# An attention and mixture-of-experts kernel: early table load, sums that hold their 1e-9, a first weight load in halves, and attention dealt out in shorter runs

## The chip, the cores and the metric

The kernel runs on one core of a Trainium2 chip, as one program. The metric is the device time of one execution in microseconds; of the kernel before there are three runs. The engines are called PE (TensorE, matrix products), ACT (ScalarE), DVE (VectorE), POOL (GpSimd) and SP (SyncE, which issues the DMAs).

## The reference

Attention over 4 batches, 8 heads, 576 positions of 64 channels, and behind it a layer of four experts over its output, weighted with given probabilities:

```python
scores = scale * np.matmul(q, k.transpose(0, 1, 3, 2))
mask_local = (rel >= 0) & (rel < stride)                       # heads 0 to 3, stride 32
mask_strided = (rel >= 0) & (pos[None, :] % stride == pos[:, None] % stride)   # heads 4 to 7
scores = np.where(masks[None, :, :, :], scores, -1000000000.0)
scores = scores - np.max(scores, axis=-1, keepdims=True)
attn = np.exp(scores)
attn = attn / (np.sum(attn, axis=-1, keepdims=True) + 1e-09)
x = np.matmul(attn, v)                                         # as 2304 rows of 512
p = domain_probs / (domain_probs.sum(-1, keepdims=True) + 1e-9)
for e in range(4):
    h = np.maximum(x @ w1[e], 0.0)                             # 512 to 1024
    out += p[:, e:e + 1] * (h @ w2[e])                         # 1024 to 512
```

## The kernel before

**Numbers.** Every fp32 operand of the expert layer is split into a high part (a copy by ACT) and a low part (source minus high part, by DVE or POOL), and each product is three products: high by high, low by high, high by low.

**Stages.** There are eight units: four experts, each with two halves of 512 hidden columns. Stage one computes attention and, in the same stretch, all eight units for the first 384 rows of x: line 752 multiplies with w1 (48 products of 384 columns for each unit), line 768 with w2 (36 of 512 columns). Stage two (from the first product of line 921) takes the next 896 rows through the units, stage three the last 1024, both with fewer products by sums of quarters (tiles s1 to s4 of the weights, t1 to t4 of x). The transforms of x for stage two (`plan_x`, line 895 and the sums of lines 667 and 670) need all of attention.

**Attention.** Sixteen pairs of heads come in the order local, strided, local, strided of each batch. A pair has two groups. For each group: scores on PE (line 494 local, 499 strided), mask and maximum on DVE (510, 513), the difference on DVE or POOL (516), the exponent on ACT (520), the sum on DVE (525 and 526 local, 528 strided), the reciprocal (529), the product with it on DVE or POOL (532), transposes on PE (556) which ACT or DVE copy out (433, 435), and products with v on PE (583 local, 591 strided). The result goes to `xh` and `xl` for the first 384 rows and to `xr1`, `xr2` for the others. In the strided tiles a 55th column holds 1e-9 and the sum reads it along; the local ones get the 1e-9 added in an instruction of its own (526).

**What sets the order.** No loop runs the work in its written order: `Plan.add` gathers operations with an engine, a length, the tokens that they read and write, and a due time; `Plan.walk` deals them out engine by engine, by the due times and by its own lengths. Pair n of attention has the due time `ZB * n` for the first four and `ZP * n` later, unit u has `Z0 + ZU * u`. On PE, products of the expert layer and attention take turns; once attention has run for `ROW` microseconds by the plan, it is the products' turn. Where PE would have nothing, `fill` puts in products of a zero tile (line 1232), of which nobody reads the result. The engines then run these fixed orders, with semaphores between them.

**Loads.** SP issues them one after another: q and k (422, 424), v (429), weights (652: a quarter of a w1 or w2 pair, 1 MB).

Of the kernel before, what the change touches and what calls it, by code (L numbers as in the profile page):

```python
# [8 lines left out]
F32 = mybir.dt.float32  # L9
# [18 lines left out]

# [4 lines left out]
class Plan:  # L33
# [5 lines left out]
    TICK = 4096 / 1200  # L39
    BUSY, WARM = 3200, 2000  # L40
    LANES, RING = 8, 2048
    DEEP = 1.3
    ROW = 1.51
    ENGINES = ("PE", "ACT", "DVE", "POOL", "SP")
    FLEX = {"VP": ("DVE", "POOL"), "AD": ("ACT", "DVE")}

# [263 lines left out]
def attn_moe_kernel(  # L310
# [48 lines left out]
    prs = const.tile([P, NTT, E], F32, name="prs")  # L359
    psums = const.tile([P, NTT], F32, name="psums")  # L360
    wz = const.tile([P, 512], BF16, name="wz")
    const.tile([P, 8], F32, name="skew")

    wt = {n: big.tile([P, 2, 2, 256], F32R, name=n) for n in QUART[:3] + ("s3",)}
    wq = {n: (t[:, 0], t[:, 1]) for n, t in wt.items()}
# [75 lines left out]
    def plan_pair(n):  # L441
# [16 lines left out]

        pmx = pm[kd][bf]

        def pmv(g0, g1):
            if kd == "S":
                return pmx[:, g0:g1, 0:W]
            a = pmx[:, P * g0 + 1:P * g0 + 2]
            return bass.AP(a.tensor, a.offset, [list(a.ap[0]), [3 * P, (g1 - g0) // 3], [P + 32, 3], [1, W]])

        def per(a, g0, g1):

# [5 lines left out]
        def rows(a, g0, g1):  # L474
            a = a[:, par, g0:g1]
            return a if kd == "S" else a.rearrange("p (v r) -> p v r", r=3)
        par = n % 2
        for gi, (g0, g1) in enumerate(GRP[kd]):
            z = zg[gi]
            ng = g1 - g0  # L480
            key = ("sc", n, "b", gi)
            nel = ng * W

            def scores(key=key, gi=gi, g0=g0, g1=g1):
                s = bank(key)
                for g in range(g0, g1):
                    o = (g - g0) * W
                    for h in range(2):
                        a = slice(64 * h, 64 * h + 64)
                        if kd == "L":  # L490
                            o0, nq, _ = QKL[gi]
                            for i in range(2):
                                t = o0 + 96 * (2 * ((g - g0) // 3) + i) + 32 * (g % 3)
                                nc.tensor.matmul(  # L494
                                    s[64 * h + 32 * i:64 * h + 32 * i + 32, o:o + W], qkv[a, t:t + 32],
                                    qkv[a, t + nq + 1:t + nq + 1 + W], start=True, stop=True)
                        else:
# [24 lines left out]
            def rsum(g0=g0, g1=g1):  # L522
                r = sm[:, par, g0:g1]
                if kd == "L":
                    nc.vector.tensor_reduce(out=rows(sm, g0, g1), in_=pmv(g0, g1), op=ALU.add, axis=AX.X)
                    nc.vector.tensor_scalar_add(out=r, in0=r, scalar1=1e-9)
                else:
                    nc.vector.tensor_reduce(out=r, in_=pmx[:, g0:g1, 0:W + 1], op=ALU.add, axis=AX.X)
                nc.vector.reciprocal(out=r, in_=r)

            def norm(e, g0=g0, g1=g1, ng=ng):
                engine(e).tensor_tensor(
                    out=pmv(g0, g1), in0=pmv(g0, g1), in1=per(sm, g0, g1), op=ALU.mult)

            tok, tm, ts = f"pm{kd}{bf}{gi}", f"mx{par}{gi}", f"sm{par}{gi}"
            dd = nel / 960 + 0.15
            vp = (dd, nel * 1.6e-3 + 0.22)
            add("PE", 0.2 + ng * (0.107, 0.116)[c > 1], scores, [f"qk{kd}{bf}{gi}"], [key, tok], z + 3, key, cols=(4, 2)[c > 1] * nel)
            add("DVE", dd, mask, [key, "mask" + kd], [tok], z + 3.2)
            add("DVE", dd, rmax, [tok], [tm], z + 3.4)  # L540
            add("VP", vp, bsub, [tm], [tok], z + 3.6)
            add("ACT", nel / 1200 + 0.2, ex, (), [tok], z + 3.8)
            add("DVE", dd + (0.45, 0.25)[c > 1], rsum, [tok], [ts], z + 4)
            add("VP", vp, norm, [ts], [tok], z + 4.2)


# [99 lines left out]
    units = [(e, f) for e in range(E) for f in range(F // FH)]  # L646
    NU = len(units)

    def load_w(which, u):
        e, f = units[u]  # L650
        src = w1[e, :, f * FH:(f + 1) * FH] if which == 1 else w2[e, f * FH:(f + 1) * FH, :]
        nc.sync.dma_start(out=raws[which], in_=src.rearrange("(k p) f -> p k f", p=P))

    def raw_quarter(i, j, which=1):
        return raws[which][:, 2 * j:2 * j + 2, 256 * i:256 * i + 256]
# [14 lines left out]
        add("VP", VP, lambda e: engine(e).tensor_tensor(out=dst(), in0=a(), in1=b(), op=ALU.add), toks, [tok], z)  # L670

    def plan_load(which, u, z):
        add("SP", 0.4, lambda: load_w(which, u), (), [f"raw{which}"], z, xfer=((2.9, 512),), lag=LAG)

    def plan_w2(z):
        for i in range(NKF):
            split(lambda i=i: raws[2][:, i, :], "raw2", lambda i=i: w2h[i], lambda i=i: w2l[i], f"w2{i}", z)

    A11, A12, A21, A22 = ((lambda i=i, j=j: raw_quarter(i, j)) for i in range(2) for j in range(2))

    def plan_quarter(src, tok, nm, z):
        split(src, tok, lambda: wq[nm][0], lambda: wq[nm][1], nm, z)

    def plan_w1_plain(z):
        for src, nm in ((A11, "a11"), (A12, "a12"), (A21, "s3"), (A22, "a22")):
            plan_quarter(src, "raw1", nm, z)

    tmp = {}

    def plan_w1(z, step, plain):  # L690

        def t(i):
            return lambda: tmp["s", i]

        if plain:
            plan_quarter(A11, "raw1", "a11", z)
        total(t(0), A21, A22, ["raw1"], "ws0", z + step)
        plan_quarter(t(0), "ws0", "s1", z + step)
        combine(t(1), t(0), A11, ["raw1", "ws0"], "ws1", z + 2 * step)
        plan_quarter(t(1), "ws1", "s2", z + 2 * step)  # L700
        if plain:
            plan_quarter(A12, "raw1", "a12", z + 3 * step)
        combine(t(2), A11, A21, ["raw1"], "ws2", z + 4 * step)
        plan_quarter(t(2), "ws2", "s3", z + 4 * step)
        if plain:
            plan_quarter(A22, "raw1", "a22", z + 5 * step)
        combine(t(0), A12, t(1), ["raw1", "ws1"], "ws0", z + 6 * step)
        plan_quarter(t(0), "ws0", "s4", z + 6 * step)


# [7 lines left out]
    def plan_keep2(u, z, step):  # L718
# [8 lines left out]
        def t(i):  # L727
            return lambda: tmp["s", i]
# [4 lines left out]
            add("SP", 0.4, lambda: nc.sync.dma_start(out=d2[u, nm], in_=late["wv"][v].bitcast(F32)), [f"wv{v}h", f"wv{v}l"], [f"d2{u}{nm}"],  # L733
                z + n * step + 2, xfer=((1.45, 128),))

        total(t(0), B21, B22, ["raw2", "late2"], "ws0", z)
        keep(0, "s1")
        combine(t(1), t(0), B11, ["raw2", "ws0"], "ws1", z + step)
        keep(1, "s2")
        combine(t(2), B11, B21, ["raw2"], "ws2", z + 2 * step)  # L740
        keep(2, "s3")
        combine(t(0), B12, t(1), ["raw2", "ws1"], "ws0", z + 3 * step)
        keep(3, "s4")

    PASS = [(i, c) for i in range(3) for c in range(NKD)]
# [430 lines left out]
    for n in range(NP):  # L1176
        plan_pair(n)
    add("SP", 0.4, load_pr, (), ["prs"], 8, xfer=((0.1, 128),))
    add("DVE", 1.0, normalize, ["prs"], ["pr"], 30)
    key = ("ps", "pr")  # L1180

    def turn_pr():
# [27 lines left out]
    for i, u in enumerate(first_order):  # L1210
# [7 lines left out]
        if u != NU - 2:  # L1218
# [3 lines left out]
        z += w1_at  # L1222
    plan_x(2, z, 2 * pm_of(2))
    add("DVE", 0.0, open_third, [f"{nm}l{j}" for nm in XOPS for j in range(2)],
        ["late3", "raw1", "raw2"] + [t for t in list(plan.writer) if isinstance(t, str) and (
            t[0] == "H" or t[:2] in ("r2", "ws", "wv", "w2") or t in [f"{x}{i}" for x in "uc" for i in range(4)])], z)
    plan_second()

# [90 lines left out]
```

## Time and profile before

| | us |
|---|---|
| three runs | 805.32, 806.19, 807.41 (median 806.19) |
| the profiled execution | 805.53 |
| its span, first to last instruction | 803.7 |
| PE busy | 794.7 (99%) |
| DVE, POOL, ACT busy | 612.9, 357.3, 330.4 |
| first product of stage two (line 921) | starts at 206.60 |
| last PE instruction ends | 799.98 |

A busy time is the time in which an engine has at least one instruction in work; on PE consecutive products overlap, so the distance from one start to the next says what a product costs, and not its own length. A product of unsplit fp32 operands (lines 494, 499, 583, 591) stands in the trace as two records: 12 instructions of line 591 are x24 there. A row in brackets such as [1.77 <-POOL pmL L532] says how long the engine stood idle before the instruction and what ended that.

### The profile page before, as it was taken

How to read it: one execution, taken by the hardware profiler on the slowest of the kernel's cores; microseconds unless marked ns; L12 is line 12 of the kernel's file. 1: busy time of each engine (PE TensorE's matmuls, PEld its weight loads, DVE VectorE, ACT ScalarE, POOL GpSimd, SP SyncE). 2: the span in 40 equal slices, each digit the busy share in tenths (PEclk: the TensorE clock that was granted, in tenths of full speed). 3: DMA queues.
4: the chain of work that ended last, by engine and by line, in shares of the span. 5: the costliest groups of instructions: out<-in, count | busy, mean ns of one | idle time of the engine just before them, and what ended most of it. 6: DMA issues, size and time to landing. Idle time of an engine off the chain costs nothing.

```text
span 803.7 us, 13270 instructions
## 1 busy us (share of the span) xinstructions
PE 794.7 (99%) x5035; PEld 678.3 (84%) x5035; DVE 612.9 (76%) x871; ACT 330.4 (41%) x617; POOL 357.3 (44%) x277
## 2 busy tenths in 40 slices
PE   8999999999999999999999999999999999999998
PEld 5888888999889898888989888888888887888886
DVE  6888886875689776868687683868687878696986
ACT  3744646443336253444526361524131414232330
POOL 5442322932276451515244361526271808071762
PEclk9999999999999999999999999999999999999999
DMA  9675433348668696967764314838384747464625
GB/s 332 221 267 213 175 113 106 105 152 293 250 261 267 261 318 222 333 200 291 262 254 131 135 51 164 298 112 302 106 287 145 257 150 256 154 217 182 184 79 184
DMA packets 70400, 166.60 MB, mean 207 GB/s; under 512 B 5152, under 2 KB 23744, under 8 KB 70336
## 3 DMA queue, kind: packets, MB, share of 16 engines
q1 hardware_dynamic: 70192, 165.63, 58.8%
q8 instruction: 40, 0.66, 0.3%
q14 instruction: 24, 0.20, 0.1%
q10 hardware_dynamic: 144, 0.11, 0.0%
HBM read 105.94 MB, written 59.79 MB: 206 GB/s over the span
## 4 chain that ended last, share of the span: by engine, by line
PE 96%; DVE 2%; DMA 1%; ACT 1%; issue 0%; POOL 0%; DVEq 0%; ACTq 0%
PE mo L921 21%; PE mo L768 18%; PE ps L921 17%; PE sc L921 15%; PE mo L752 8%; PE sc L768 5%; PE ps L768 5%; PE ps L556 2%; PE ps L591 1%; PE sc L499 1%; DMA ring<-d23s 1%; PE sc L494 1%; PE ps L583 1%; PE mo L1232 1%; DVE wv L663 0%
## 5 line engine op out<-in xcount | busy, mean ns | idle before, releaser
L986 POOL TENSOR_TENSOR q<-q,q 128x512 f32<-128x512 f32 x41 | 60.9, 1494 | 143.2 <-DVE q L955 142.4
L768 PE MATMUL mo<-w2t,h 128*128 128x512 f32 x336 | 80.8, 389 | 0.0
L768 PEld LDWEIGHTS mo<-w2t,h 128*128 128x128 f32 x336 | 63.1, 188 | 13.0
L768 PE MATMUL mo<-w2t,hs 128*128 128x512 f32 x288 | 70.5, 396 | 0.0
L759 DVE SCALAR_TENSOR_TENSOR h<-c,h 128x448 fp32r<-128x448 f32 x48 | 61.3, 1305 | 2.4 <-ACT h L756 0.8
L768 PEld LDWEIGHTS mo<-w2t,hs 128*128 128x128 f32 x288 | 52.8, 188 | 11.0
L662 ACT ACTIVATE w2t<-raw 128x512 fp32r<-128x512 f32 x60 | 37.1, 630 | 41.9 <-PE mo L768 21.8
L663 POOL TENSOR_TENSOR a<-raw,a 128x512 fp32r<-128x512 f32 x19 | 29.8, 1570 | 52.8 <-DVE c L1124 48.0
L1035 DVE TENSOR_TENSOR acc<-sc,acc 128x512 f32<-128x512 f32 x58 | 39.2, 686 | 17.3 <-PE sc L921 17.2
L952 DVE TENSOR_TENSOR q<-ps,v 128x512 f32<-128x512 f32 x48 | 33.1, 690 | 24.9 <-PE ps L921 24.7
L777 DVE SCALAR_TENSOR_TENSOR acc<-mo,pr,acc 128x512 f32<-128x512 f32 x45 | 33.5, 745 | 22.3 <-PE mo L768 22.1
L943 ACT ACTIVATE v<-mo 128x512 f32<-128x512 f32 x48 | 28.6, 595 | 48.2 <-PE mo L921 48.2
L663 POOL TENSOR_TENSOR w2t<-raw,w2t 128x512 fp32r<-128x512 f32 x19 | 26.7, 1412 | 44.8 <-ACT w2t L662 44.8
L752 PE MATMUL mo<-xh,a 128*128 128x384 f32 x192 | 45.6, 341 | 0.0
L955 DVE SCALAR_TENSOR_TENSOR q<-q,pb 128x512 f32<-128x512 f32 x48 | 42.8, 892 | 1.6
L662 ACT ACTIVATE wv<-tmp 128x512 fp32r<-128x512 f32 x32 | 20.1, 632 | 54.6 <-POOL tmp L670 10.5
L768 PE MATMUL ps<-w2t,h 128*128 128x512 f32 x168 | 40.4, 389 | 0.0
L768 PE MATMUL sc<-w2t,h 128*128 128x512 f32 x168 | 40.4, 389 | 0.0
L981 ACT ACTIVATE Tb11h<-q 128x512 fp32r<-128x512 f32 x16 | 10.0, 628 | 71.5 <-DVE q L955 71.5
L663 DVE TENSOR_TENSOR w2t<-raw,w2t 128x512 fp32r<-128x512 f32 x41 | 35.1, 883 | 5.1 <-ACT w2t L662 5.1
L986 DVE TENSOR_TENSOR q<-q,q 128x512 f32<-128x512 f32 x23 | 32.7, 1421 | 6.7 <-POOL Tb21l L982 6.5
L768 PEld LDWEIGHTS sc<-w2t,h 128*128 128x128 f32 x168 | 31.5, 188 | 6.5
(270 smaller groups left out, 2109.0 us busy)
## 6 DMA issues: line engine op xcount, KB each, us to landing
raw<-in_w SPq DMA_DIRECT2D x30, 1024.0 KB, 6.1
qkS<-in_qk_strided SPq DMA_DIRECT2D x16, 329.0 KB, 6.5
out<-acc SPq DMA_DIRECT2D x18, 256.0 KB, 2.0
qkL<-in_qk_local SPq DMA_DIRECT2D x8, 400.0 KB, 6.5
vstL<-in_v_local SPq DMA_DIRECT2D x8, 384.0 KB, 7.0
vstS<-in_v_strided SPq DMA_DIRECT2D x8, 384.0 KB, 7.3
pb<-dp SPq DMA_DIRECT2D x5, 512.0 KB, 7.2
d17s<-s SPq DMA_DIRECT2D x4, 512.0 KB, 4.0
```

What stands on the lines that cost most here:

```text
L662: add("ACT", 0.62, lambda: nc.scalar.activation(out=hi(), in_=src(), func=AF.Copy), need, [name + "h"], z)
L663: add("VP", VP, lambda e: engine(e).tensor_tensor(out=lo(), in0=src(), in1=hi().bitcast(F32), op=ALU.subtract), need + [name + "h"], [name ...
L752: nc.tensor.matmul(pt[:, 0:TA], w[:, c % 2, (f % 2) * P:(f % 2) * P + P], (xl if i == 1 else xh)[c], start=j == 0, stop=j == 11)
L759: nc.vector.scalar_tensor_tensor(out=dst(), in0=src(), scalar=0.0, in1=hi().bitcast(F32), op0=ALU.max, op1=ALU.subtract)
L768: nc.tensor.matmul(pt, ht[f][:, ts], wt[f][:, cs], start=j == 0, stop=j == 11)
L777: nc.vector.scalar_tensor_tensor(out=a, in0=pt, scalar=sc, in1=a, op0=ALU.mult, op1=ALU.add)
L921: nc.tensor.matmul(pt, a[i == 2][:, j, f * P:f * P + P], skewed(b[i == 1][j], TH), start=bool(first) and n == 0, stop=True, skip_group_che ...
L943: add("ACT", TH2 / 1200 + 0.18, lambda: nc.scalar.activation(out=late["u"][i], in_=held[key][:, 0:TH2], func=AF.Copy), [key, "late3"], [f" ...
L952: add("DVE", DD, lambda: nc.vector.tensor_tensor(out=q(), in0=src(), in1=late["u"][i], op=ALU.add), [key, f"u{i}", "late3"], [tok], min(zz ...
L955: add("DVE", DD, lambda: nc.vector.scalar_tensor_tensor(out=q(), in0=q() if from_q else src(), scalar=0.0, in1=late["p"][:, c * TH2:c * TH ...
L986: add("VP", VP, lambda e: engine(e).tensor_tensor(out=dst[0](), in0=a[0](), in1=b[0](), op=ALU.subtract), [a[1], b[1]], [dst[1]], zz - 2.4)
L1035: add("DVE", DD, lambda i=i, key=key: nc.vector.tensor_tensor(out=acc[i], in0=held[key][:, 0:TH2], in1=acc[i], op=ALU.add), [key], tok, zd)
```

## The change

The masks' function now issues one exponent of a single zero element (`warm`), so the table load of ACT, which stands ahead of the first exponent, comes before the first scores. The local tiles get 1e-9 in the column before each window of 63, and the sum reads 64 columns; the addition of line 526 goes. The first load of w1 is two loads of half the size, each with its own token, and its quarters are split in the order a11, s3, a12, a22. The planner's numbers differ: attention's due times lie 6.11 apart instead of 11.46 and those of the units 10.62 instead of 27.0, and a run of attention may last 0.6 instead of 1.51.

```diff
-ZB, ZP = 4.82, 11.46
+ZN = 35.4
+ZR0, ZR1 = 26.0, 19.9
+ZB, ZP = 4.82, 6.11
 ZD = 2.0
-VZ = 3.77
-Z0, ZU = 24.03, 27.0
-
-LEAD = 11.15
-LAG = 2.35
+VZ = 2.9
+Z0, ZU = 26.25, 10.62
+
+LEAD = 13.23
+LAG = 3.28
...
-    DEEP = 1.3
-    ROW = 1.51
+    DEEP = 1.49
+    ROW = 0.6
...
-            a = pmx[:, P * g0 + 1:P * g0 + 2]
-            return bass.AP(a.tensor, a.offset, [list(a.ap[0]), [3 * P, (g1 - g0) // 3], [P + 32, 3], [1, W]])
+            a = pmx[:, P * g0 + 1 - eps:P * g0 + 2 - eps]
+            return bass.AP(a.tensor, a.offset, [list(a.ap[0]), [3 * P, (g1 - g0) // 3], [P + 32, 3], [1, W + eps]])
...
-                    nc.vector.tensor_reduce(out=rows(sm, g0, g1), in_=pmv(g0, g1), op=ALU.add, axis=AX.X)
-                    nc.vector.tensor_scalar_add(out=r, in0=r, scalar1=1e-9)
+                    nc.vector.tensor_reduce(out=rows(sm, g0, g1), in_=pmv(g0, g1, 1), op=ALU.add, axis=AX.X)
...
-        add("SP", 0.4, lambda: load_w(which, u), (), [f"raw{which}"], z, xfer=((2.9, 512),), lag=LAG)
+        toks = [f"raw{which}{j}" for j in range(2)]
+        if u or which == 2:
+            add("SP", 0.4, lambda: load_w(which, u), (), toks, z, xfer=((2.9, 512),), lag=LAG)
+            return
+        for j in range(2):
+            add("SP", 0.4, lambda j=j: load_w(which, u, slice(2 * j, 2 * j + 2)), (), [toks[j]], Z0 - (ZR0, ZR1)[j], xfer=((1.45, 256),), lag=LAG)
...
-        for src, nm in ((A11, "a11"), (A12, "a12"), (A21, "s3"), (A22, "a22")):
-            plan_quarter(src, "raw1", nm, z)
+        for src, nm, j in ((A11, "a11", 0), (A21, "s3", 0), (A12, "a12", 1), (A22, "a22", 1)):
+            plan_quarter(src, f"raw1{j}", nm, z)
...
         nc.scalar.dma_start(out=both, in_=c_masks)
+        nc.scalar.activation(out=warm[:, 0:1], in_=wz[:, 0:1], func=AF.Exp)
...
-    add("DVE", 1.0, normalize, ["prs"], ["pr"], 30)
+    add("DVE", 1.0, normalize, ["prs"], ["pr"], ZN)
...
         for t in pm["L"]:
             nc.gpsimd.memset(t, 0.0)
+            a = t[:, 0:1]
+            nc.gpsimd.memset(bass.AP(a.tensor, a.offset, [list(a.ap[0]), [3 * P, 3], [P + 32, 3], [1, 1]]), 1e-9)
```

PE's order in the middle of stage one, before: scores, six products of line 768 (written as four rows), the strided product with v of both groups of a pair (24 instructions of line 591), six products of line 768.

```order
L494 MATMUL sc<-qkL_235 32x63 x24
L556 MATMUL ps<-ident,pmL_242 128x128 x3
L768 MATMUL mo<-w2t,hs_225 128x512 x2
L768 MATMUL mo<-w2t,hs_229 128x512
L768 MATMUL mo<-w2t,hs_226 128x512 x2
L768 MATMUL mo<-w2t,hs_230 128x512
L591 MATMUL ps<-pTS,vstS_241 64x54 x24
L768 MATMUL mo<-w2t,hs_223 128x512 x2
L768 MATMUL mo<-w2t,hs_227 128x512
L768 MATMUL mo<-w2t,hs_224 128x512 x2
L768 MATMUL mo<-w2t,hs_228 128x512
L556 MATMUL ps<-ident,pmL_242 128x128 x6
```

The same engine and the same kind of place in the changed kernel, whose lines 592 and 774 are 591 and 768 before.

```order
L501 MATMUL sc<-qkS_236 64x54 x12
L774 MATMUL mo<-w2t,hs_225 128x512 x2
L774 MATMUL mo<-w2t,hs_229 128x512
L774 MATMUL mo<-w2t,hs_226 128x512 x2
L774 MATMUL mo<-w2t,hs_230 128x512
L592 MATMUL ps<-pTS,vstS_241 64x54 x12
L774 MATMUL mo<-w2t,hs_223 128x512 x2
L774 MATMUL mo<-w2t,hs_227 128x512
L774 MATMUL mo<-w2t,hs_224 128x512 x2
L774 MATMUL mo<-w2t,hs_228 128x512
L592 MATMUL ps<-pTS,vstS_241 64x54 x12
L774 MATMUL mo<-w2t,hs_225 128x512 x2
```

The two groups of the strided product with v stand apart, with six products between them. The last piece of attention stands ahead of eight blocks of whole rounds of lines 752 and 768 before, and ahead of four in the changed kernel.

ACT's order at the program's start, before; pmL and pmS are attention's local and strided tiles, pTL a transposed one.

```order
L1162 DMA both<-c_masks 128x432
L520 ACT_TABLE_LOAD
L520 ACTIVATE pmL_242<-pmL_242 128x2x3x63
L520 ACTIVATE pmL_242<-pmL_242 128x3x63
L433 ACTIVATE pTL<-ps 128x384 x2
```

The same stretch in the changed kernel, whose lines 522 and 435 are 520 and 433 before.

```order
L1168 DMA both<-c_masks 128x432
L1169 ACT_TABLE_LOAD
L1169 ACTIVATE warm<-wz 128x1
L522 ACTIVATE pmL_242<-pmL_242 128x2x3x63
L522 ACTIVATE pmL_242<-pmL_242 128x3x63
L435 ACTIVATE pTL<-ps 128x384 x2
```

The table load now belongs to the exponent of the zero tile, which waits for no scores.

## Rows read from the trace of the kernel before

**Rows 1.** The page: engines' busy time; PE's busy tenths in 40 equal slices.

```profile
PE 794.7 (99%) x5035; PEld 678.3 (84%) x5035; DVE 612.9 (76%) x871; ACT 330.4 (41%) x617; POOL 357.3 (44%) x277
...
PE   8999999999999999999999999999999999999998
```

**Rows 2.** Timeline of PE, head: start, busy us, instruction, [idle before, releaser].

```profile
1.19 4.56 PE L1232 MATMUL mo<-wz 128*128 128x512 bf16 x11 [1.19 <-DVE wz L1235]
5.68 1.20 PE L494 MATMUL sc<-qkL 64*32 64x63 f32 x72
...
10.07 0.61 PE L1232 MATMUL mo<-wz 128*128 128x512 bf16 x2
12.45 0.88 PE L556 MATMUL ps<-ident,pmL 128*128 128x128 f32 x6 [1.77 <-POOL pmL L532]
...
15.64 1.04 PE L1232 MATMUL mo<-wz 128*128 128x512 bf16 x4
```

**Rows 3.** Timeline of all engines, 8 to 12 us.

```profile
8.61 1.28 ACT L520 ACT_TABLE_LOAD   x1 [8.61 <-DVE pmL L516]
...
11.03 0.17 DVE L526 TENSOR_SCALAR sm<-sm 128x6 f32<-128x6 f32 x1
11.24 0.19 DVE L529 RECIPROCAL sm<-sm 128x6 f32<-128x6 f32 x1
```

**Rows 4.** Timeline of PE, 61 to 128 us: starts of blocks.

```profile
61.77 1.43 PE L591 MATMUL ps<-pTS,vstS 54*64 54x54 f32 x48
63.12 1.67 PE L768 MATMUL mo<-w2t,hs 128*128 128x512 f32 x6
64.63 0.82 PE L556 MATMUL ps<-ident,pmL 128*128 128x128 f32 x6
65.38 0.53 PE L494 MATMUL sc<-qkL 64*32 64x63 f32 x24
...
66.68 1.65 PE L768 MATMUL mo<-w2t,hs 128*128 128x512 f32 x6
68.26 1.21 PE L583 MATMUL ps<-pTL,vstL 128*64 128x96 f32 x24
69.40 0.91 PE L499 MATMUL sc<-qkS 64*64 64x54 f32 x24
...
73.61 1.63 PE L768 MATMUL mo<-w2t,hs 128*128 128x512 f32 x6
75.17 1.43 PE L591 MATMUL ps<-pTS,vstS 54*64 54x54 f32 x48
...
115.44 1.62 PE L768 MATMUL mo<-w2t,hs 128*128 128x512 f32 x6
116.91 0.49 PE L556 MATMUL ps<-ident,pmL 128*128 128x128 f32 x3
117.33 0.91 PE L591 MATMUL ps<-pTS,vstS 54*64 54x54 f32 x24
118.17 0.96 PE L752 MATMUL mo<-xh,a 128*128 128x384 f32 x4
...
127.30 0.55 PE L583 MATMUL ps<-pTL,vstL 128*64 128x96 f32 x8
127.78 0.55 PE L556 MATMUL ps<-ident,pmS 128*128 128x128 f32 x3
```

**Rows 5.** Timeline of PE, late in stage one and at its end.

```profile
148.70 1.55 PE L768 MATMUL mo<-w2t,hs 128*128 128x512 f32 x6
...
156.90 0.87 PE L752 MATMUL mo<-xh,a 128*128 128x384 f32 x4
...
206.60 0.57 PE L921 MATMUL mo<-b11h,a 128*128 128x448 f32 x2
```

**Rows 6.** Timelines of ACT and POOL: last copy of attention, last transform.

```profile
133.02 1.58 ACT L638 ACTIVATE xr<-ps 128x324 f32<-128x324 f32 x2 [1.03 <-PE ps L591]
...
159.38 1.60 POOL L895 TENSOR_TENSOR t4l<-tmp,t4h 128x448 fp32r<-128x448 f32 x1
```

More of the change, by code (lines that the diff above doesn't have):

```diff
@@ L361, in attn_moe_kernel @@
     wz = const.tile([P, 512], BF16, name="wz")
-    const.tile([P, 8], F32, name="skew")
+    warm = const.tile([P, 8], F32, name="warm")
     wt = {n: big.tile([P, 2, 2, 256], F32R, name=n) for n in QUART[:3] + ("s3",)}
@@ L459, in plan_pair, with pmv @@
         pmx = pm[kd][bf]
-        def pmv(g0, g1):
+        def pmv(g0, g1, eps=0):
             if kd == "S":
                 return pmx[:, g0:g1, 0:W]
-            a = pmx[:, P * g0 + 1:P * g0 + 2]
-            return bass.AP(a.tensor, a.offset, [list(a.ap[0]), [3 * P, (g1 - g0) // 3], [P + 32, 3], [1, W]])
+            a = pmx[:, P * g0 + 1 - eps:P * g0 + 2 - eps]
+            return bass.AP(a.tensor, a.offset, [list(a.ap[0]), [3 * P, (g1 - g0) // 3], [P + 32, 3], [1, W + eps]])
         def per(a, g0, g1):
@@ L542, in plan_pair @@
             add("ACT", nel / 1200 + 0.2, ex, (), [tok], z + 3.8)
-            add("DVE", dd + (0.45, 0.25)[c > 1], rsum, [tok], [ts], z + 4)
+            add("DVE", dd + 0.25, rsum, [tok], [ts], z + 4)
             add("VP", vp, norm, [ts], [tok], z + 4.2)
@@ L647, in attn_moe_kernel, with load_w @@
     NU = len(units)
-    def load_w(which, u):
+    def load_w(which, u, ks=slice(0, NKD)):
         e, f = units[u]
         src = w1[e, :, f * FH:(f + 1) * FH] if which == 1 else w2[e, f * FH:(f + 1) * FH, :]
-        nc.sync.dma_start(out=raws[which], in_=src.rearrange("(k p) f -> p k f", p=P))
+        nc.sync.dma_start(out=raws[which][:, ks], in_=src.rearrange("(k p) f -> p k f", p=P)[:, ks])
     def raw_quarter(i, j, which=1):
@@ L672, in plan_load @@
     def plan_load(which, u, z):
-        add("SP", 0.4, lambda: load_w(which, u), (), [f"raw{which}"], z, xfer=((2.9, 512),), lag=LAG)
+        toks = [f"raw{which}{j}" for j in range(2)]
[4 more added lines that the diff above has]
+            add("SP", 0.4, lambda j=j: load_w(which, u, slice(2 * j, 2 * j + 2)), (), [toks[j]], Z0 - (ZR0, ZR1)[j], xfer=((1.45, 256),), lag=LAG)
     def plan_w2(z):
         for i in range(NKF):
-            split(lambda i=i: raws[2][:, i, :], "raw2", lambda i=i: w2h[i], lambda i=i: w2l[i], f"w2{i}", z)
+            split(lambda i=i: raws[2][:, i, :], f"raw2{i // 2}", lambda i=i: w2h[i], lambda i=i: w2l[i], f"w2{i}", z)
     A11, A12, A21, A22 = ((lambda i=i, j=j: raw_quarter(i, j)) for i in range(2) for j in range(2))
@@ L695, in plan_w1 @@
         if plain:
-            plan_quarter(A11, "raw1", "a11", z)
-        total(t(0), A21, A22, ["raw1"], "ws0", z + step)
+            plan_quarter(A11, "raw10", "a11", z)
+        total(t(0), A21, A22, ["raw10", "raw11"], "ws0", z + step)
         plan_quarter(t(0), "ws0", "s1", z + step)
-        combine(t(1), t(0), A11, ["raw1", "ws0"], "ws1", z + 2 * step)
+        combine(t(1), t(0), A11, ["raw10", "ws0"], "ws1", z + 2 * step)
         plan_quarter(t(1), "ws1", "s2", z + 2 * step)
         if plain:
-            plan_quarter(A12, "raw1", "a12", z + 3 * step)
-        combine(t(2), A11, A21, ["raw1"], "ws2", z + 4 * step)
+            plan_quarter(A12, "raw11", "a12", z + 3 * step)
+        combine(t(2), A11, A21, ["raw10"], "ws2", z + 4 * step)
         plan_quarter(t(2), "ws2", "s3", z + 4 * step)
         if plain:
-            plan_quarter(A22, "raw1", "a22", z + 5 * step)
-        combine(t(0), A12, t(1), ["raw1", "ws1"], "ws0", z + 6 * step)
+            plan_quarter(A22, "raw11", "a22", z + 5 * step)
+        combine(t(0), A12, t(1), ["raw11", "ws1"], "ws0", z + 6 * step)
         plan_quarter(t(0), "ws0", "s4", z + 6 * step)
@@ L734, in keep @@
                 z + n * step + 2, xfer=((1.45, 128),))
-        total(t(0), B21, B22, ["raw2", "late2"], "ws0", z)
+        total(t(0), B21, B22, ["raw20", "raw21", "late2"], "ws0", z)
         keep(0, "s1")
-        combine(t(1), t(0), B11, ["raw2", "ws0"], "ws1", z + step)
+        combine(t(1), t(0), B11, ["raw20", "raw21", "ws0"], "ws1", z + step)
         keep(1, "s2")
-        combine(t(2), B11, B21, ["raw2"], "ws2", z + 2 * step)
+        combine(t(2), B11, B21, ["raw20", "raw21"], "ws2", z + 2 * step)
         keep(2, "s3")
-        combine(t(0), B12, t(1), ["raw2", "ws1"], "ws0", z + 3 * step)
+        combine(t(0), B12, t(1), ["raw20", "raw21", "ws1"], "ws0", z + 3 * step)
         keep(3, "s4")
@@ L1224, in attn_moe_kernel @@
     add("DVE", 0.0, open_third, [f"{nm}l{j}" for nm in XOPS for j in range(2)],
-        ["late3", "raw1", "raw2"] + [t for t in list(plan.writer) if isinstance(t, str) and (
+        ["late3", "raw10", "raw11", "raw20", "raw21"] + [t for t in list(plan.writer) if isinstance(t, str) and (
             t[0] == "H" or t[:2] in ("r2", "ws", "wv", "w2") or t in [f"{x}{i}" for x in "uc" for i in range(4)])], z)
```

## The prediction

> **What bounds the kernel now.** I read the page's head first, then TensorE's (PE's) timeline in three places, then the rows of all engines where PE waits. The head shows PE busy for 99% of the span against 76% of VectorE (DVE), and PE's busy share by slice is nine tenths or more in all slices but the first and the last [rows 1]. So after the first 20 us only what PE itself does can change the time; in them waits can. PE's head shows the large one: 1.77 us of idle time ahead of the first transposes at 12.45, ended by GpSimd's (POOL's) product with the reciprocal [rows 2]. The rows of the other engines tell why: the exponent needs a table load of 1.28 us on ScalarE (ACT), which starts only when its input is ready at 8.61; behind it stand the sum, the addition of 1e-9 (11.03) and the reciprocal (11.24) [rows 3].
>
> PE's order changes in stage one alone, that is ahead of the first product of line 921 at 206.60 [rows 5]. Behind it the order on PE is the old one, so I leave the 597 us there as they are.
>
> **The change part by part: what a switch costs.** From a block's start to the next block's start is what it costs PE [rows 4]. "Small" stands for scores and products with v, which use a part of the array; "products" are those of lines 752 and 768.
>
> - Six products of line 768 inside a run take 8.20 / 36 x 6 = 1.37 us [rows 5]. With small blocks on both sides they take 68.26 - 66.68 = 1.58: 0.21 more. With small ahead and transposes behind 64.63 - 63.12 = 1.51 (0.12 more, as line 752 gives a little less); transposes ahead and small behind 75.17 - 73.61 = 1.56 (0.19); transposes on both sides 116.91 - 115.44 = 1.47 (0.10). No idle time stands in those rows.
> - Runs of products next to attention, of these four kinds, counted in the order: before 8, 10, 9, 6 (33 runs), after 23, 15, 5, 7 (50). That is 1.7 + 1.2 + 1.7 + 0.6 = 5.2 us before and 4.8 + 1.8 + 1.0 + 0.7 = 8.3 after: **+3.1**.
> - The strided product with v takes 63.12 - 61.77 = 1.35 for both groups together, and 118.17 - 117.33 = 0.84 for one alone: 0.33 for a split pair. Of 8 pairs 1 is split before, 6 after: **+1.6**.
> - The local product with v takes 69.40 - 68.26 = 1.14 with 12 instructions and 127.78 - 127.30 = 0.48 with 4: 0.083 for each and 0.15 for a block. Of 8 pairs 2 are in two blocks before, 5 after: **+0.5**.
> - Transposes with products ahead and small behind take 117.33 - 116.91 = 0.42 for three and 65.38 - 64.63 = 0.75 for six: 0.11 each and 0.09 for the block. There are 11 of these before, 15 after: 0.4; the other neighbours I take at 0.1: **+0.5**.
> - Fillers (line 1232): 18 before, 15 after, at 0.22: **-0.65**.
>
> Sum: +5.05 us of PE's own work.
>
> The Trainium skill bears on the price: "TensorEngine Tiling (Array Packing)", section Tiling Modes, says that changing the tiling mode drains TensorE, and changing only the tile does not. By that rule full-array transposes beside full-array products would cost nothing at the edge; the rows have 0.10 for a run between transposes. By the rule alone, 15 runs before and 12 after would lose their 0.1 behind transposes, and the sum would be 0.3 higher. The measurement decides.
>
> **The waits.** At the same costs the blocks of stage one before sum to 199.1 us: products 132.4 (384 x 0.174 and 288 x 0.228, from the rounds of [rows 5]: 49.70 / 3 = 16.57 for 48 and 36 of them, 8.20 of it the 36), their switches 5.2, scores 23.0, products with v 20.6, transposes 14.0, fillers 3.9. PE starts at 1.19, and its first 11 fillers take 5.68 - 1.19 = 4.5 us instead of 2.4 [rows 2]. So 206.6 - 1.2 - 2.1 - 199.1 leaves **4.2 us of waits** in stage one:
>
> - 0.9 of it lies ahead of 10.07, where scores wait for a bank and their data: 4.39 us from 5.68 for blocks of 3.5 [rows 2]. No order changes there. It stays.
> - The early load takes 1.28 out of the first chain, and the sum that holds its 1e-9 takes 11.24 - 11.03 = 0.21 [rows 3]. PE's time at 12.45 between the end of its two fillers' cost (10.50) and the transposes is 1.95; 0.45 of it stays. What is late next is the same product on POOL, at about 10.95. ACT, which is idle until 8.61, hides the load.
> - The next chain (strided exponent, sum, reciprocal, product) lies behind the four fillers at 15.64 [rows 2]. One filler is left there, and the strided product with v now comes ahead of the first product of line 752. I take 0.85 of waiting, a little over the three fillers (0.65) that are gone: a filler stands where PE has nothing else, and its leaving alone makes no operand earlier.
> - The small waits between 20 and 40 us fall in an order that no longer stands; I take zero.
>
> 2.2 us stay; the ends are 0.9 (only what the change doesn't touch) and 4.2 (nothing gained).
>
> The other edits I cost at nothing. The other 15 additions go from a DVE on which PE hardly waits after 20 us. POOL's two fills of the 1e-9 column come before 8 us, where it has no other work. The first weight load in halves brings the first half earlier, where PE has transposes ahead of it anyway; the second half falls behind a load of v, and the first w2 load behind five loads of q, k and v on SP's queue. I bound these from -0.3 (the waits between 20 and 40 us) to +0.5 (a load that is late by one of them) and take zero. The later normalization has until the first accumulation.
>
> **Sum.** 5.05 - (4.2 - 2.2) = +3.05. On the profiled execution's 805.5 that is 808.6; the median of the three runs lies 0.66 higher, so I predict 809.2. With the ends of the waits it is +1.75 (807.9) to +5.05 (811.2).
>
> **The rivals.**
>
> 1. *The waits go, the switches stay.* Only the 0.9 is left, and the other edits give their 0.3: +1.45, 807.6, which can't be told from no change. For it: three fillers fewer may mean that PE has operands there. Against: the strided chain has no shorter step than before.
> 2. *The switches are waits in disguise* (not slower). The 0.10 to 0.33 at the edges would be PE waiting for operands or banks that a longer spread brings in time. Then the 5.7 of switching isn't paid, and 0.65 and 2.0 are saved: 802.9 on the profile's basis, 803.5. Its place is the edges of runs from 40 to 165 us, and it decides when more than about half of the 5.7 goes. Against it: no idle time in those rows, and like neighbours cost alike [rows 4].
> 3. *Stage two starts late.* The last piece of attention is copied at 133.02, and the transforms that stage two needs run on DVE and POOL until 159.38 + 1.60 = 160.98 [rows 6]: 28 us, ready 45.6 ahead of 206.60 [rows 5]. In the new order attention ends two rounds of 16.57 nearer to the end, which leaves 12.5 us. If the weights of the last two rounds, split on the same engines, stretch the 28 us to 45, PE waits 5: 811.2 + 3 = 814. Against: the slack is near half of the whole.
>
> **How the numbers follow.** The three runs spread over 0.3%, so 2.4 us is about what can be told from no change. The forecast gets 0.65, rival 1 0.18, rival 2 0.08, rival 3 0.09. Of the forecast's +1.75 to +5.05 about a tenth of the chance lies under 2.4. Slower: 0.59 + 0.09 = 0.68; the same: 0.18 + 0.06 = 0.24; faster: 0.08. The range goes from 806.3, below rival 1, to 813.0, into rival 3; what is left out is rival 2 and the worst of rival 3. The forecast's own range is 807.9 to 811.5.
>
> **What would show it.** Right: the first line 921 at 209 to 211 instead of 206.6; the table load ahead of 2 us, the first transposes by 11; six products between small blocks still at 1.58 and half a strided product at 0.84; the 597 us behind it unchanged to half a us. Wrong: cheaper edges and a sooner line 921 (rival 2), PE idle at the first products of line 921 (rival 3), or new waits between 18 and 45 us, where I take none.

## The result: slower by 0.73%, 811.15 us

Five runs of the changed kernel gave 810.33 to 812.93 us (median 811.15), five of the kernel before beside them 805.32 to 807.41 (median 806.19). The ratio on record is 1.0073, 95% interval [1.006, 1.0085]; the two medians stand 4.96 us apart, 0.62%, near the lower end of it. The forecast was 809.2 with a range of 806.3 to 813.0. The profiled execution took 810.69 us against 805.53: 5.16 more.

**The page after.** Busy times of the engines, and PE's busy tenths in 40 equal slices.

```profile
PE 800.3 (99%) x5032; PEld 679.0 (84%) x5032; DVE 605.2 (75%) x861; ACT 329.3 (41%) x614; POOL 356.5 (44%) x277
...
PE   8999999999999999999999999999999999999998
```

PE is busy 5.6 us longer than in [rows 1] and the others are not. As before, PE's work or a wait of PE is what can move the end.

**PE's head, against [rows 2].** Timeline of PE: start, busy us, instruction, idle time before it and what ended that.

```profile
1.19 4.88 PE L1239 MATMUL mo<-wz 128*128 128x512 bf16 x11 [1.19 <-DVE wz L1242]
5.99 1.34 PE L496 MATMUL sc<-qkL 64*32 64x63 f32 x72
...
10.54 0.60 PE L1239 MATMUL mo<-wz 128*128 128x512 bf16 x2
11.52 0.88 PE L557 MATMUL ps<-ident,pmL 128*128 128x128 f32 x6 [0.37 <-POOL pmL L533]
...
19.16 0.51 PE L758 MATMUL mo<-xh,a 128*128 128x384 f32 x2
20.20 0.34 PE L758 MATMUL mo<-xl,a 128*128 128x384 f32 x1 [0.53 <-issue]
```

The wait ahead of the first transposes is 0.37 us instead of 1.77. But the first scores start 0.31 later, since the 11 fillers ahead of them take 4.88 us instead of 4.56, and 0.53 us of idle time stands at 20.20 within the first run of products, with "issue" as its cause: the profile shows nothing that PE waited for.

**Why the head is shorter, against [rows 3].** Timeline of ACT and DVE: the table load and the sum.

```profile
1.17 1.28 ACT L1169 ACT_TABLE_LOAD   x1 [1.17 <-PEq L1296]
9.10 0.52 ACT L522 ACTIVATE pmL<-pmL 128x378 f32<-128x378 f32 x1 [6.43 <-DVE pmL L518]
...
9.71 0.55 DVE L527 TENSOR_REDUCE sm<-pmL 128x6 f32<-128x384 f32 x1
10.30 0.19 DVE L530 RECIPROCAL sm<-sm 128x6 f32<-128x6 f32 x1
```

**The blocks' prices, against [rows 4].** Timeline of PE, starts of blocks. Lines 592, 584 and 774 are 591, 583 and 768 before.

```profile
52.31 0.91 PE L592 MATMUL ps<-pTS,vstS 54*64 54x54 f32 x24
53.15 0.61 PE L758 MATMUL mo<-xh,s 128*128 128x384 f32 x2
...
59.32 1.64 PE L774 MATMUL mo<-w2t,hs 128*128 128x512 f32 x6
60.80 0.49 PE L557 MATMUL ps<-ident,pmL 128*128 128x128 f32 x3
...
67.22 1.66 PE L774 MATMUL mo<-w2t,hs 128*128 128x512 f32 x6
68.82 0.55 PE L584 MATMUL ps<-pTL,vstL 128*64 128x96 f32 x8
69.30 0.55 PE L557 MATMUL ps<-ident,pmS 128*128 128x128 f32 x3
```

Half a strided product costs 0.84, six products between small blocks 1.60, a third of a local product 0.48, each as before. Six products between transposes cost 1.48 (1.47 in [rows 4]).

**The end of stage one, against [rows 5, 6].** Timelines of PE, ACT (attention's last copy) and DVE (the last transform).

```profile
210.43 0.57 PE L927 MATMUL mo<-b11h,a 128*128 128x448 f32 x2
```

```profile
170.50 0.78 ACT L639 ACTIVATE xr<-ps 128x324 f32<-128x324 f32 x1 [1.68 <-PE ps L592]
```

```profile
198.55 1.24 DVE L901 TENSOR_TENSOR t4l<-tmp,t4h 128x448 fp32r<-128x448 f32 x1
```

Stage two starts 3.83 us later than before (206.60). Attention's last copy ends 36.7 us later (171.28 instead of 134.60), and the transforms are ready at 199.79, 10.6 us ahead of their use. What lies behind the first product of stage two is 808.89 - 210.43 = 598.46 us against 597.14: 1.33 more, which the prediction did not have. So 3.83 + 1.33 = 5.16.

Busy time of the engines from PE's first instruction to stage two, before and after (stretch, its length, then PE's busy time and count, those of PEld, DVE, ACT and POOL, PEclk, DMA share, GB/s):

```profile
1.19:206.60 205.41, 202.39 (x2347) 174.23 (x2348) 156.08 (x303) 103.38 (x215) 84.85 (x87) 1.00 0.57 199
1.19:210.43 209.24, 207.79 (x2345) 175.08 (x2345) 153.05 (x293) 102.74 (x212) 86.09 (x88) 1.00 0.54 188
```

PE works 5.40 us more there and stands idle for 1.45 us instead of 3.02.

**Where the 1.33 us are.** Timelines of PE, ACT and SP in stage two of the changed kernel; the line of PE had no wait in the kernel before.

```profile
260.40 0.67 PE L927 MATMUL ps<-t4h,a 128*128 128x448 f32 x2 [1.78 <-ACT u L1117]
```

```profile
238.11 1.41 ACT L663 ACTIVATE wv<-tmp 128x512 fp32r<-128x512 f32 x2 [3.62 <-POOL tmp L671]
246.70 0.63 ACT L663 ACTIVATE wv<-tmp 128x512 fp32r<-128x512 f32 x1 [7.18 <-DMA d20s<-wv]
```

```profile
236.74 0.32 SPq L719 DMA_DIRECT2D d10s<-s  x1
237.11 0.43 SPq L653 DMA_DIRECT2D raw<-in_w  x1
239.50 11.98 SPq L739 DMA_DIRECT2D d20s<-wv  x4
```

The same queues in the kernel before: ACT, then SP.

```profile
233.51 0.63 ACT L662 ACTIVATE wv<-tmp 128x512 fp32r<-128x512 f32 x1 [3.40 <-DVE tmp L670]
240.33 0.63 ACT L662 ACTIVATE wv<-tmp 128x512 fp32r<-128x512 f32 x1 [4.81 <-DMA d20s<-wv]
```

```profile
229.47 0.47 SPq L652 DMA_DIRECT2D raw<-in_w  x1
232.74 0.32 SPq L713 DMA_DIRECT2D d10s<-s  x1
235.42 9.68 SPq L733 DMA_DIRECT2D d20s<-wv  x4
```

There are two wv buffers; the third split must wait until the first store has read its buffer. Before, SP issued the 1 MB load of raw1 ahead of the last d10s store; after, that store comes first, waits for its split, and the load goes out 2.4 us ahead of the wv store. That store then lands 7.1 us after its issue instead of 4.8, ACT stands 7.18 us, its copies of PE's results (`u`) come late, and PE waits for a bank. SP's order is not the only one that differs: the sum that the first split waits for is DVE's before (line 670) and POOL's after (line 671).

### The profile page after: what moved, and what is told of

Its sections match the earlier page's. It is cut to its first block, busy times and chain, and to the rows that moved or that the text cites. A ratio compares the mean times of both kernels' runs of the same rounds, so it can differ in the third digit from the quotient of the medians.

```text
span 808.9 us, 13177 instructions
## 1 busy us (share of the span) xinstructions
PE 800.3 (99%) x5032; PEld 679.0 (84%) x5032; DVE 605.2 (75%) x861; ACT 329.3 (41%) x614; POOL 356.5 (44%) x277
## 4 chain that ended last, share of the span: by engine, by line
PE 91%; POOL 3%; DVE 2%; issue 2%; DMA 1%; ACT 0%; DVEq 0%; POOLq 0%; ACTq 0%
PE mo L927 19%; PE mo L774 17%; PE ps L927 15%; PE sc L927 14%; PE mo L758 9%; PE ps L774 4%; PE sc L774 4%; PE ps L557 2%; PE ps L592 2%; PE sc L501 1%; PE ps L584 1%; PE sc L496 1%; DMA d20s<-wv 1%; PE mo L1239 1%; DMA d27s<-wv 1%
## 5 line engine op out<-in xcount | busy, mean ns | idle before, releaser
L774 PE MATMUL mo<-w2t,hs 128*128 128x512 f32 x288 | 74.0, 402 | 0.0
L765 DVE SCALAR_TENSOR_TENSOR h<-c,h 128x448 fp32r<-128x448 f32 x48 | 58.8, 1253 | 2.2 <-ACT h L762 0.8
L664 POOL TENSOR_TENSOR w2t<-raw,w2t 128x512 fp32r<-128x512 f32 x23 | 31.7, 1386 | 36.2 <-ACT w2t L663 30.5
L774 PEld LDWEIGHTS ps<-w2t,h 128*128 128x128 f32 x168 | 31.5, 188 | 6.5
```

The source lines that it names most:

```text
L664: add("VP", VP, lambda e: engine(e).tensor_tensor(out=lo(), in0=src(), in1=hi().bitcast(F32), op=ALU.subtract), need + [name + "h"], [name ...
L765: nc.vector.scalar_tensor_tensor(out=dst(), in0=src(), scalar=0.0, in1=hi().bitcast(F32), op0=ALU.max, op1=ALU.subtract)
L774: nc.tensor.matmul(pt, ht[f][:, ts], wt[f][:, cs], start=j == 0, stop=j == 11)
```

## The experiments

All were timed in five rounds beside the kernel before. "Stage two" is the start of its first product in the profiled execution, "behind" the span from there.

| kernel | median us | ratio to before, 95% | stage two | behind |
|---|---|---|---|---|
| before | 805.15 to 806.19 | 1 | 206.60 | 597.14 |
| after | 811.15 | 1.0073 [1.006, 1.0085] | 210.43 | 598.46 |
| a_row151: after, ROW 1.51 | 806.55 | 1.0014 [1.0005, 1.0022] | 206.88 | 597.66 |
| a_row4: after, ROW 4.0 | 805.42 | 1.0007 [0.9997, 1.0018] | 204.73 | 598.26 |
| a_swap: after, load ahead of store | 809.91 | 1.0061 [1.0045, 1.0077] | 211.02 | 596.30 |
| a_fix: a_row4 and a_swap | 804.67 | 0.9989 [0.998, 0.9999] | 206.55 | 596.35 |
| a_halfone: after, stage two's load whole | 811.68 | 1.0068 [1.0051, 1.0085] | 209.55 | 601.66 |
| b_row06: before, ROW 0.6 | 811.69 | 1.0086 [1.0073, 1.0099] | 213.69 | 595.58 |
| b_swap: before, load behind store | 805.36 | 1.0003 [0.9994, 1.0012] | 206.72 | 596.42 |
| e_headkeep: before, both head edits | 804.49 | 0.9991 [0.9983, 1.0] | 205.54 | 596.44 |
| e_warm: before, early table load | 804.19 | 0.9986 [0.9977, 0.9995] | 206.03 | 596.22 |
| k_row4: e_headkeep, ROW 4.0 | 802.61 | 0.9971 [0.996, 0.9981] | 204.22 | 596.19 |

### ROW alone: a_row151, b_row06, a_row4

```diff
-    ROW = 0.6
+    ROW = 1.51      # a_row151; 4.0 in a_row4; b_row06 sets 0.6 in the kernel before
```

> The changed kernel with one number put back: ROW from 0.6 to 1.51. Every other number and edit of the change stays. PE then has 33 runs of products in stage one instead of 50, with 15 fillers as after. Switch theory: PE's own work in stage one falls by the price of 17 switches and of the split value blocks, 5.2 us (204.2 to 199.0 by the block prices of the trace of before), so the first product of line 927 comes at 205.2 us (210.43 after), what lies behind it stays 598.5 us, and the time is 806.0 us. Waits theory (the price of a switch is PE standing for a slower engine, so that it comes back at another place): line 927 begins at 208.5 us or later and the time is 809 us or more. Due-time theory (the stretched due times of the units and of the value blocks make the loss, not the length of a turn): 810.5 to 811.5 us, as after.

> The kernel before with one number changed: ROW from 1.51 to 0.6. It has neither the early table load nor the sums with their 1e-9, the first weight load is whole, all due times are the old ones. 53 runs of products instead of 33, 18 fillers as before. Switch theory: PE's own work in stage one rises by 5.4 us (199.1 to 204.5 by the block prices), line 921 begins at 212.0 us (206.60 before), 597.1 us behind it, time 811.6 us. Waits theory: below 809 us, since the same work waits at fewer places for more. Due-time theory: 806 us, as before.

> The changed kernel with one number changed: ROW from 0.6 to 4.0. All its other numbers and edits stay, the late place of the raw1 load on SP too. 23 runs of products, 15 fillers. Switch theory: PE's own work in stage one 197.3 us by the block prices (204.2 after, 199.0 with 1.51), so 6.9 us less than after and 1.7 us less than with 1.51: ratio to before 0.9985 to 1.000. Waits theory: not below the version with 1.51 (ratio 1.0014).

ROW carries most of the loss. From after to a_row151 the ratio falls by 0.0059, 4.8 us (switch theory 5.2), with all stretched due times in place, so the due-time theory falls. The two profiled executions lie 3.94 us apart. PE's own work in stage one falls by 5.36 us (202.43 against 207.79, 5.2 expected), but its idle time rises by 1.81 to 3.26, so stage two starts at 206.88 and not at 205.2. In b_row06 the one number makes the kernel before 0.86% slower, 6.9 us (5.4 expected), and stage two starts at 213.69 (212.0 expected). The waits theory, with 809 us or more for a_row151 and less than 809 for b_row06, is wrong on both. The excess in b_row06 is a wait, though: its idle time in stage one is 4.42 us against 3.02 before. The last 36 products of line 768 took 9.66 us instead of 8.2, the 36 before the last round of line 752 8.75. Timeline of PE in b_row06, busy time by engine in its last three stretches (36, 48 and 36 products), and stage one whole, of b_row06 and of a_row151:

```profile
189.88 5.96 PE L768 MATMUL mo<-w2t,hs 128*128 128x512 f32 x25 [0.25 <-DVE hs L759]
...
207.90 5.95 PE L768 MATMUL mo<-w2t,hs 128*128 128x512 f32 x25 [0.39 <-DVE hs L759]
```

```profile
core 0: us, PE busy (x) PEld busy (x) DVE busy (x) ACT busy (x) POOL busy (x), PEclk, DMA share, GB/s
186.93:195.68 8.75, 8.50 (x37) 6.69 (x37) 7.08 (x8) 2.76 (x6) 7.58 (x7) 1.00 0.67 250
195.68:204.03 8.35, 8.35 (x50) 8.35 (x49) 8.35 (x10) 4.68 (x9) 6.02 (x4) 1.00 0.26 87
204.03:213.69 9.66, 9.17 (x38) 6.52 (x37) 6.25 (x10) 2.54 (x5) 1.74 (x1) 1.00 1.00 320
...
1.19:213.69 212.50, 208.08 (x2345) 174.30 (x2348) 151.51 (x300) 102.54 (x211) 93.66 (x94) 1.00 0.53 185
...
1.19:206.88 205.69, 202.43 (x2342) 174.24 (x2345) 155.11 (x297) 102.20 (x214) 78.31 (x82) 1.00 0.56 198
```

DVE is busy for the whole of the next-to-last stretch, with transforms for stage two until 200.50 + 1.71 = 202.21 (line 895), and splits the last `hs` too late: some 2 us of PE in all (9.66 + 8.75 - 16.4).

a_row4 starts stage two 2.15 us earlier than a_row151 (1.7 expected), of which the times show 0.6 with overlapping intervals. 0.99 of the 2.15 is the shorter time of its first 11 fillers (3.88 against 4.87 us), and a_fix, with the same stage one and 4.88 us of fillers, starts stage two at 206.55 (204.7 expected). The ratio of 1.0007 lies above the 0.9985 to 1.000 of the switch theory and below the 1.0014 of the waits theory: this run decides between neither. PE waited 0.72 and 0.63 us for `hs` at 147.68 and 149.29 there.

### The head alone: e_headkeep, e_warm

```diff
+        nc.scalar.activation(out=warm[:, 0:1], in_=wz[:, 0:1], func=AF.Exp)      # both
-                    nc.vector.tensor_scalar_add(out=r, in0=r, scalar1=1e-9)      # e_headkeep
...
```

What is left out of e_headkeep here is the wider sum and the column of 1e-9, as in the change.

> The kernel before with two edits of the change alone: the early table load, and the sums with their 1e-9 inside (one VectorE instruction in place of two). The planner's lengths are left as they were, so PE has the same instructions in the same order as before. If the early work was on the path as the prediction had it: of the 1.77 us wait ahead of the first transposes all but 0.45 us goes, line 921 begins at 205.2 us (206.60 before), time 804.8 us. If what the start gains is lost again at the next wait of stage one: 806 us. If the 597.1 us behind line 921 react to an earlier start: other than 804.8 by as much.

> The kernel before with the early table load alone (the sums keep their second VectorE instruction); PE has the same instructions in the same order as before. Path theory: the wait of 1.77 us ahead of the first transposes falls to about 0.7 us, less what a later first score takes; it was 5.99 us in each of the four runs with the early load and 5.68 and 5.42 us in the two without, so the first scores again at 6.0 us, line 921 at 205.8 us, time 0.7 to 0.9 us below before (ratio 0.9989 to 0.9991). If the later first score is only the landing of its loads and not the table load: 5.4 to 5.7 us, and 1.1 to 1.3 us below before. If the start is hidden by later waits: no difference.

PE's order is that of before in both. Stage two starts 1.06 us earlier in e_headkeep, 0.57 in e_warm, and the times are 0.7 us (0 to 1.4) and 1.1 us (0.4 to 1.9) below before: a small gain. e_warm gives what was expected (0.7 to 0.9), e_headkeep half of its 1.4, and the two cannot be told apart. The wait ahead of the transposes fell to 0.58 us in e_headkeep, but the first scores started at 6.00 there. I took that for an effect of the table load when e_warm was planned; the later runs refute it: with the early load they started at 5.00 (a_row4), 5.25 (k_row4), 5.58 (a_halfone) and at 5.99 or 6.00 in six runs; without it at 5.42, 5.68 and 5.79. What differs is the time of the 11 fillers ahead of them, which read no load. Weight loads (PEld) and fillers in after, then in a_row4:

```profile
5.00 0.15 PEld L1239 LDWEIGHTS <-wz 128*128 128x128 bf16 x1 [0.28 <-issue]
...
1.19 3.88 PE L1239 MATMUL mo<-wz 128*128 128x512 bf16 x11 [1.19 <-DVE wz L1242]
...
4.05 0.53 PEld L1239 LDWEIGHTS <-wz 128*128 128x128 bf16 x3 [0.17 <-issue]
```

In after the fillers start 0.40 to 0.43 us apart to the last, as 512 columns at 1.2 GHz take; in a_row4 they do so up to 3.72, and from 4.05 on the last ones stand 0.22 apart, the clock's upper level. In the six runs at 5.99 or 6.00 none of the 11 is at 0.22. So the start of the first scores follows the moment at which the clock rose, and it differs by run. The column PEclk has 1.00 there in all of them, so this is read from the distances alone.

### SP's order: a_swap, b_swap, a_fix, a_halfone

```diff
-        out.sort(key=lambda x: x[:2])
+        out.sort(key=lambda x: x[:2]); at = [x[1] for x in out]; x = out.pop(at.index(1024)); out.insert([x[1] for x in out].index(941), x)
```

1024 is the raw1 load and 941 the d10s4 store; b_swap moves the load behind the store in the kernel before. a_halfone makes the changed kernel's two half loads of stage two one again (`if u or which == 2 or z > 60`).

> The changed kernel with one SP instruction moved by one place: the 1 MB load of raw1 that after issues behind the store of d10s4 (237.11 us) goes ahead of it, where before has it. All else, the order of every other engine included, is the same. Theory (the load right ahead of the wv stores makes the first of them land after 7.1 us instead of 4.8, ScalarE's next wv split waits 7.2 us instead of 4.8, its u copies come late, and PE stands 1.78 us at 260.4): the wait at 260.4 goes, 597.1 to 597.4 us behind the first product of line 927 instead of 598.5, time 809.8 us. Rival (the stall comes from where the unit of stage two begins against the transfers, or from the load of unit 0 in two halves, not from this one place): 598.5 us behind it and 811 us as after.

> The kernel before with one SP instruction moved by one place, the other way round: the 1 MB load of raw1 that before issues ahead of the store of d10s4 (229.47 us) goes behind it, right ahead of the wv stores, where the changed kernel has it. All else is the same. Theory of SP's order: ScalarE's wait at its third wv split grows from 4.8 to about 7 us, PE stands 1 to 1.8 us near 256 us that it does not stand before, 598.1 to 598.9 us behind line 921 instead of 597.1, time 1.0 to 1.8 us above before (ratio 1.0012 to 1.0022). Rival (the stall comes from the new order of the other engines): no stall near 256 us, ratio 1.000.

> The changed kernel with two repairs: ROW 4.0 instead of 0.6 (23 runs of products instead of 50), and the raw1 load ahead of the store of d10s4 on SP. Both causes as separate terms: the run with ROW 4.0 alone had 598.26 us behind the first product of line 927 with a stall of 1.66 us at 255.1; that stall goes as it went with ROW 0.6, so 596.2 to 596.6 us behind it, the first product at 204.7 us as there, and the time 1.4 to 1.9 us below the run with ROW 4.0 alone: ratio to before 0.9983 to 0.9990. Rival (the gain from the place of the load depends on the turns of stage one, or the stall moves to another store): ratio as with ROW 4.0 alone, 1.0007.

> The changed kernel with one SP instruction less: the first w1 load of unit 0 stays in two halves in stage one, but the load of the same unit in stage two (204.48 and 205.85 us after) is one whole load again; the order of all engines is otherwise the same, the raw1 load stays behind the store of d10s4. It asks why the first wv store lands after 7.1 us here (7.0 and 7.7 in the two other runs of this kind) but after 5.6 us in the kernel before with the load moved to the same place. If the halves in stage two are the reason: it lands after 5.6 us or less, no stall at 260 us, 596.2 to 597.1 us behind the first product of line 927, 809.5 us. If not: 7 us, a stall of 1.0 to 1.8 us at 260 us, 598 to 598.5 us, 811 us as after.

In the changed kernel the place of the load is the cause of the stall: in a_swap every other engine has the order of after. With it ahead (a_swap, a_fix) 596.30 and 596.35 us lie behind; with it behind the store 598.46, 597.66 and 598.26 (after, a_row151, a_row4), with stalls of 1.78, 1.03 and 1.66 us of the same product. ACT in a_swap:

```profile
238.50 1.41 ACT L663 ACTIVATE wv<-tmp 128x512 fp32r<-128x512 f32 x2 [4.00 <-POOL tmp L671]
244.32 0.63 ACT L663 ACTIVATE wv<-tmp 128x512 fp32r<-128x512 f32 x1 [4.42 <-DMA d20s<-wv]
```

By the times alone it is weaker: a_swap is 1.0 us below after and a_fix 1.4 below a_row4 (1.4 to 1.9 expected), each with overlapping intervals. And 597.14 us behind in the kernel before are high for it: e_headkeep and e_warm, with its orders behind stage one, have 596.44 and 596.22, without the wait of 0.69 us that stands at 682.77 in before.

b_swap went against the theory: in the kernel before, the same move costs nothing. The store landed after 5.6 us (4.8 before), ACT waited 5.58, and PE did not stall. So the place of the load does harm only with the rest of the changed plan, in which ACT, DVE and POOL have other orders in stage two's first unit too; no run parts these from it. a_halfone shows that the halved load is not that rest: the store landed after 6.9 us and PE stood 1.79 us. Why the store lands after 5.6 us in one plan and 7 in the other, with issues 2.3 to 2.4 us behind the load in both, stays open.

a_halfone's 601.66 us are 3.2 more than after's; 1.27 of them lie behind PE's last product, and its profiled execution shows something else. Granted clock of PE (column PEclk), then PE's timeline right behind the stall:

```profile
core 0: us, PE busy (x) PEld busy (x) DVE busy (x) ACT busy (x) POOL busy (x), PEclk, DMA share, GB/s
256.00:259.00 3.00, 1.83 (x10) 1.37 (x8) 2.90 (x6) 1.54 (x3) 0.40 (x1) 1.00 1.04 373
259.00:262.00 3.00, 2.38 (x10) 2.17 (x11) 2.78 (x5) 2.28 (x6) 2.48 (x2) 0.85 1.03 274
262.00:265.00 3.00, 3.00 (x11) 2.70 (x10) 2.17 (x4) 1.84 (x4) 0.00 (x0) 0.58 0.88 267
265.00:268.00 3.00, 3.00 (x16) 2.61 (x15) 2.29 (x4) 1.63 (x3) 1.87 (x2) 1.00 1.03 420
```

```profile
259.62 0.68 PE L927 MATMUL ps<-t4h,a 128*128 128x448 f32 x2 [1.79 <-ACT u L1117]
260.13 0.57 PE L927 MATMUL ps<-t4l,a 128*128 128x448 f32 x2
260.54 0.56 PE L927 MATMUL ps<-t4h,a 128*128 128x448 f32 x2
...
262.30 0.95 PE L927 MATMUL mo<-t4h,a 128*128 128x448 f32 x2
263.04 0.95 PE L927 MATMUL ps<-b22h,s 128*128 128x448 f32 x2
```

Two products take 0.74 us from start to start (262.30 to 263.04) where 0.41 is usual (260.13 to 260.54): the clock is at the lower of its two levels, 1.2 instead of 2.4 GHz, for some 3 us behind the stall. In after, a_row151 and a_row4 the same stall had no such sequel.

### A faster version: k_row4

```diff
-    ROW = 1.51
+    ROW = 4      # and the two edits of e_headkeep
```

> The kernel before with the early table load, the sums with their 1e-9 inside (planner's lengths as before), and ROW 4.0 instead of 1.51: turns of attention and of products longer, not shorter. 26 runs of products instead of 33, 18 fillers. Switch theory: PE's own work in stage one 196.3 us by the block prices (199.1 before), 2.8 us less, and 0.7 to 1.4 us from the start as in the run of those two edits alone: time 3.5 to 4.2 us below before (ratio 0.9948 to 0.9957). Waits theory (longer turns make PE wait for the softmax or for the transforms, as the 2.0 us of waits in the last products with ROW 0.6 on the kernel before hint): the gain is eaten, 0.5 to 1.5 us below before.

It is faster than both kernels: 0.29% below before, 2.3 us (1.5 to 3.2), between the two theories. PE's busy time in stage one is 198.80 us, 3.59 less than before (0.42 of it in the first fillers), and its idle time 1.21 more, so a part of the gain came back as waits. Two idle times of PE:

```profile
14.11 1.04 PE L582 MATMUL ps<-pTL,vstL 128*64 128x96 f32 x19 [1.27 <-issue]
...
60.62 0.52 PE L555 MATMUL ps<-ident,pmL 128*128 128x128 f32 x3 [0.42 <-ACT xr L637]
```

## Why the prediction was right, and where it was too low

**PE's own work: right.** PE's busy time in stage one grew by 5.40 us. 0.32 of it is the slower start of the 11 fillers (4.88 instead of 4.56), which leaves 5.08 against +5.05. The blocks shown above have their old prices, so the sum is right in its terms too. The Trainium skill ("TensorEngine Tiling (Array Packing)", Tiling Modes) has TensorE drained where the tiling mode changes; the prediction read from it that edges between transposes and products are free. The 1.48 us at 59.32 has their price of 0.1 again, so the measurement stands against that reading.

**The waits of stage one: right in kind, 0.8 too hopeful.** 2.0 us were to go; 1.57 of idle time went, and the fillers took 0.32 more: 5.08 + 0.32 - 1.57 = 3.83. The first chain gave what it should (0.37 us of idle time left), though the transposes came at 11.52 and not by 11. The terms mis-sized are the fillers, whose time the prediction left as it was, and the 0.53 at 20.20: a new wait between 18 and 45 us, where it took none. The first is luck: it hangs on when the clock rose. The second may not be: idle time with "issue" stands near 20 us in five of the six profiles of the changed kernel and its variants (0.24 to 0.74 us; a_row4 has none) and in none of before, b_row06, b_swap, e_headkeep and e_warm; its cause stays open. Three profiles with this same stage one have stage two at 209.55, 210.43 and 211.02, so 0.8 us is within what one execution scatters.

**The step that failed** is "Behind it the order on PE is the old one, so I leave the 597 us there as they are." PE's order was the old one, but SP's was not, nor were those of ACT, DVE and POOL in the first unit, and PE waits for what they and SP's transfers release. Between the two profiles it cost 1.33 us (2.16 between after and a_swap): waits of 1.78 and 0.29 (at 260.40 and 687.79) against 0.38 and 0.69 before (at 219.15 and 682.77) make 1.0 of it; the other 0.3 I can't place. The order hung on little: the planner of the kernel before, run by itself, puts the load at 230.70 and the store at 231.10, that of the changed kernel at 229.50 and 228.79.

**The rivals.** Rival 1 (the waits go, +1.45 in all) fell: stage two alone came 3.83 us later. Rival 2 (switches are waits in disguise) fell: equal blocks cost the same in both profiles, and with ROW alone the loss went and came, as busy time of PE. Rival 3 did not occur, but its slack had shrunk to 10.6 us (12.5 predicted), and in b_row06, where DVE was full up to 204.03, PE did wait some 2 us for it, at the last `hs` and not at stage two's first product.

Against the forecast of 809.2 the median is 1.95 higher: 0.8 from stage one, 1.3 from stage two, 0.2 less from the basis. The two upper ends that the prediction gives for its forecast, 811.2 and 811.5, don't agree; the median lies below both.

## What to carry to other kernels

On an engine that is always busy, count the edges between kinds of work before moving any: here a run of products between attention blocks costs 0.1 to 0.2 us and a split block 0.15 to 0.33, so 17 more runs and the blocks that they split were 5 us; longer turns gained less than was counted, since waits ate a part. When a planner deals out the work, compare the order of every queue to the program's end, and not only the bound engine's: in the changed kernel two DMAs in the other order, 27 us behind the last moved product, cost some 2 us in the profiles, and in the kernel before the same exchange cost nothing.

## What the runs showed that was not expected

A stall of PE of 1.79 us was in one execution followed by some 3 us at half clock, 1.6 us on top of it, by the starts of the products against those of after; three other executions with a stall there had none. The Trainium skill ("TensorE: Matmul & The Clock Gate", Part 1: The HAM clock gate) says that an idle PE loses its fast clock and that sustained work brings it back; the granted clock of 0.58 from 262 to 265 us agrees in that one run, the 1.00 behind the stalls of the other three shows that a stall of 1.0 to 1.8 us alone does not decide it. Nor is such a loss bound to this stall: of 71 executions of the kernel before, whose profile has no stall there, 13 have a mean granted clock of 0.998 instead of 0.999 or 1.000, and their median is 1.2 to 1.5 us above that of the others beside them; where in these the clock fell is not on record.

And the first scores of the twelve profiled programs started between 5.00 and 6.00 us, though all have the same 11 fillers ahead of them: a tenth of a per cent of the span lies in when PE's clock rises at the start.
